# Sixteen weight-block sums of a seven-product first layer: from VectorE subtractions to ScalarE copies plus adding DMA transfers

## The chip, the core and the metric

The kernel runs on one core of one Trainium2 chip. The metric is the device time of one execution in microseconds. Five engines work side by side, each through its own list of instructions in order: TensorE (matrix products, PE in the profile, with its weight loads as PEld), VectorE (DVE), ScalarE (ACT), GpSimd (POOL) and SyncE (SP). They wait for each other through semaphores. SP and POOL also issue DMA transfers here; all of these run on the core's 16 DMA engines.

## What is computed

Block-sorted attention (4 batches, 8 heads, sequence 768, head size 64) is followed by four small two-layer networks ("experts") whose outputs are mixed by token weights. The change is in the experts' first layer, `x @ w1[e]`:

```python
def _moe_ref(x, domain_probs, w1, w2):
    p = domain_probs / (domain_probs.sum(-1, keepdims=True) + 1e-09)
    out = np.zeros((N, D), dtype=np.float32)
    for e in range(E):
        h = np.maximum(x @ w1[e], 0.0)
        out += p[:, e:e + 1] * (h @ w2[e])
```

Here x, the attention's output, has 3072 rows (tokens) of 512, each w1[e] is 512 x 1024, each w2[e] 1024 x 512.

## The kernel before, in words

The 3072 tokens are worked through in 12 groups of 256, three ("chunks") to a batch. Groups 0 to 5 (batches 0 and 1) compute the first layer with plain products (line 768). In their chunks the attention of the next batch is woven in. Groups 6 to 11 (`last_chunk`, from G0 = 6 on) have no attention left and compute the first layer of each expert with seven products of half-size blocks instead of eight (the Strassen-Winograd scheme, `seven`, line 1022). For that each weight matrix is cut into four blocks, a11, a12, a21, a22 (each 128 partitions x 1024 f16 values, 2 x 512), and four sums of blocks per expert are wanted once, before group 6: s1 = a21 + a22, s3 = a11 - a21, s2 = s1 - a11, s4 = a12 - s2. The first three go into blocks of the tile `arena`, whose earlier contents (keys, values, queries, mixing matrices of the attention) are no longer needed by then; s4 overwrites a21 in the weight tile itself, so it must wait until the plain first layer of group 5 has read a21. The matching sums of the tokens (t1 to t4) are made by `token_sums` for each group.

The products of `seven` are called by number: p1 (a11 x b11) and p5 (s1 x t1) of expert 0 are issued by `last_begin` near the end of group 5, p6 (s2 x t2) in the middle of that group's last product; p7 uses s3, p4 uses a22 and p3 uses s4. They accumulate in PSUM banks X, Z, Q.

What sets the order of the work: every engine's list is in program order, and the program is an order written out by hand. `chunk(b, c, slot)` calls `slot()` after each of eight first-layer groups (slots 0 to 7) and then after each product of the second layer (slots 8 to 14). At each slot, `PLANS` names attention steps (`st_v`, `st_k`, `st_s`, `st_a`, `st_x`, ...) and, in batch 1, `PLAN_A` names weight sums: an entry (c, n, e, m) is "chunk c, slot n, expert e, sum m", run after the attention steps of the slot. In the second layer of a chunk of batch 1 (lines 826 to 854) ScalarE empties the PSUM banks: line 831 copies bankA to p1 (in the list after slot 9), 834 bankQ to p5, 839 bankA to u2, 844 bankC to ob; TensorE overwrites bankA twice more in the chunk, and each time needs the copy ahead of it to be done. Attention step `st_s` ends in exponentials on ScalarE (line 413), `st_v` in a copy (line 360) and six SP transfers that build vs (line 368), which `st_a` (line 441 on TensorE, 422 and 423 on VectorE) reads; `st_x` issues DMA transposes (line 457).

The sums themselves are made by `input_sums`, one VectorE instruction each (line 968). Fifteen are in `PLAN_A`; the s4 of expert 3 is made in two halves inside group 6 (`late_sums`, lines 1107, 1108 and 1180). In groups 6 to 11 GpSimd does half of the weighting of the hidden layer (line 1045), and ScalarE the rectifying before it (line 1044) and the copies 1052, 1059 and 1067.

Of the kernel before, what the change touches and what calls it, by code (L numbers as in the profile page):

```python
# [12 lines left out]
ALU = mybir.AluOpType  # L13
# [4 lines left out]
def kernel(  # L18
# [11 lines left out]
    nc = tc.nc  # L30
# [916 lines left out]
    def a_block(n):  # L947
        return arena[:, ds(n * AW, AW)].rearrange("p (k f) -> p k f", k=2)


    A_ORDER = (6, 7, 8, 0, 1, 2, 3, 4, 5, 9, 10, 11)
    As = []
    for e in range(E):
        w, hk, hf = w1sb[e], NKC // 2, FF // 2
        As.append({
            "a11": w[:, 0:hk, 0:hf], "a12": w[:, hk:NKC, 0:hf],
            "a21": w[:, 0:hk, hf:FF], "a22": w[:, hk:NKC, hf:FF], "s4": w[:, 0:hk, hf:FF],
            "s1": a_block(A_ORDER[3 * e]), "s3": a_block(A_ORDER[3 * e + 1]), "s2": a_block(A_ORDER[3 * e + 2]),
        })

    def input_sums(e, n, half=None):
        a = As[e]
        dst, x, y, op = (
            ("s1", "a21", "a22", ALU.add), ("s3", "a11", "a21", ALU.subtract),
            ("s2", "s1", "a11", ALU.subtract), ("s4", "a12", "s2", ALU.subtract),
        )[n]
        part = slice(None) if half is None else slice(half, half + 1)
        nc.vector.tensor_tensor(a[dst][:, part], a[x][:, part], a[y][:, part], op)

    Bs = {}  # L970

    G0 = 2 * (R // 2)
    GN = B * (R // 2)

    def token_sums(g):

        b, c = divmod(g, R // 2)
        xT = xTs[b].rearrange("p k i x -> p k (i x)")
        blk = lambda k, t: xT[:, ds(2 * k, 2), ds((2 * c + t) * P, P)]
        t3 = kTs[g % 2][:, 0:3 * 2 * P].rearrange("p (n k x) -> p n k x", n=3, k=2)  # L980
        t = Bs[g] = {
            "b11": blk(0, 0), "b12": blk(0, 1), "b21": blk(1, 0), "b22": blk(1, 1),
            "t1": t3[:, 0], "t2": t3[:, 1], "t3": t3[:, 2],
            "t4": wide[g % 2][:, 0:2 * P].rearrange("p (k x) -> p k x", k=2),
        }
        for dst, x, y in (("t1", "b12", "b11"), ("t2", "b22", "t1"), ("t3", "b22", "b12"), ("t4", "b21", "t2")):
            nc.vector.tensor_tensor(t[dst], t[x], t[y], ALU.subtract)

    last = {}

# [31 lines left out]
    def seven(g, e):  # L1022

        a, t, pb = As[e], Bs[g], pbs[divmod(g, R // 2)]
        X, Z, u2, u3, t22, t12 = [last[nm][e % 2] for nm in ("X", "Z", "u2", "u3", "t22", "t12")]
        X, Z, Q = X[:], Z[:], last["Q"][e][:]
        tt = nc.vector.tensor_tensor

        def product(dst, lhs, rhs, first=False):
            for f in range(KH):  # L1030
                for k in range(2):
                    nc.tensor.matmul(  # L1032
                        dst[:, ds(f * P, P)], a[lhs][:, k, ds(f * P, P)], t[rhs][:, k, :],
                        start=(first and f == 0 and k == 0), stop=(f == KH - 1 and k == 1), skip_group_check=True,
                    )

        def finish(i, j, src):
            nc.vector.scalar_tensor_tensor(
                out=Hb[:, e, ds(i * KH, KH), ds(j * P, P)], in0=src.rearrange("p (f x) -> p f x", f=KH), scalar=0.0,
                op0=ALU.max, in1=pb[:, ds(e, 1), ds(j * P, P)].broadcast_to([P, KH, P]), op1=ALU.mult,  # L1040
            )

        def finish2(i, j, src):
            nc.scalar.activation(src, src, AF.Relu, bias=0.0, scale=1.0)  # L1044
            nc.gpsimd.tensor_tensor(  # L1045
                Hb[:, e, ds(i * KH, KH), ds(j * P, P)], src.rearrange("p (f x) -> p f x", f=KH),
                pb[:, ds(e, 1), ds(j * P, P)].broadcast_to([P, KH, P]), ALU.mult,
            )

        def p1():  # L1050
            product(Z, "a11", "b11", True)
            nc.scalar.copy(X, Z)  # L1052

        def p5():
            product(Q, "s1", "t1", True)

        def p6():
            product(X, "s2", "t2")
            nc.scalar.copy(u2, X)  # L1059

        def p2():
            product(Z, "a12", "b21")
            finish(0, 0, Z)

        def p7():
            product(X, "s3", "t3")
            nc.scalar.copy(u3, X)  # L1067
            tt(t22, Q, u3, ALU.add)  # L1068

        def p4():  # L1070
            product(X, "a22", "t4")
            finish(1, 0, X)

        def p3():
            product(Q, "s4", "b22")
            tt(t12, Q, u2, ALU.add)  # L1076

        return {
            1: p1, 2: p2, 3: p3, 4: p4, 5: p5, 6: p6, 7: p7,
            22: lambda: finish2(1, 1, t22), 12: lambda: finish2(0, 1, t12),  # L1080
        }
# [6 lines left out]
    def last_chunk(g):  # L1088
# [6 lines left out]
        for e in range(1, E):  # L1095
            now, prev = prs[e], prs[e - 1]
            now[1]()
            prev[7]()
            if e > 1:
                prs[e - 2][12]()  # L1100
            now[5]()
            now[2]()
            now[6]()
            prev[22]()
            prev[4]()
            prev[3]()
            for n in late_sums.pop((g, e), ()):
                input_sums(*n)
        now[7]()
        prev[12]()  # L1110

# [47 lines left out]
        if not final:  # L1159
            token_sums(g + 1)  # L1160
# [12 lines left out]


    PLAN_A = [
        (1, 11, 0, 0), (1, 13, 0, 1), (2, 1, 0, 2), (2, 3, 1, 0), (2, 5, 1, 1), (2, 7, 1, 2),
        (2, 8, 2, 0), (2, 9, 2, 1), (2, 10, 2, 2), (2, 10, 0, 3), (2, 11, 1, 3), (2, 11, 3, 0), (2, 12, 2, 3),
        (2, 13, 3, 1), (2, 14, 3, 2),
    ]
    late_sums = {(G0, 1): [(3, 3, 0)], (G0, 2): [(3, 3, 1)]}  # L1180


    mk0 = mix_half("k", 0, 0, psm, 8)
# [109 lines left out]
    for b in range(2):  # L1293
        for c in range(R // 2):
            done = (1, 2) if (b, c) == (0, 0) else ()
            at = [2 * len(done)]

            def slot(b=b, c=c, at=at):
                here = (c, at[0])
                for cc, n, f, *args in PLANS[b]:  # L1300
                    if (cc, n) == here:
                        f(*args)
                if b:
                    for cc, n, e, m in PLAN_A:
                        if (cc, n) == here:
                            input_sums(e, m)
                    if here == (R // 2 - 1, 7):
                        prepare_last()
                    if here == (R // 2 - 1, 12):
                        token_sums(G0)  # L1310
                    if here == (R // 2 - 1, 13):
                        last_begin(G0)
                at[0] += 1

            chunk(b, c, slot, done)
    for g in range(G0, GN):
        last_chunk(g)
# [28 lines left out]
```

The softmax here doesn't subtract the row's maximum and nothing guards it: scores larger than these inputs give would overflow.

## Time and profile before

| | |
|---|---|
| median of 4 runs | 365.7 us (364.48 to 366.11) |
| the profiled execution | 365.25 us, span 363.2 us |
| TensorE busy / VectorE / ScalarE / GpSimd | 354.8 / 280.1 / 157.6 / 117.4 us |
| the 17 instructions of line 968 | from 178.9 to 220.3 us; a whole one 0.68 us, the two halves 1.08 and 0.81 |
| granted TensorE clock | 1.000 |

The span goes from the first to the last instruction of one profiled execution; its time is a little longer. "Busy" is the time in which an engine has an instruction under way; register, semaphore and DMA-issuing instructions are not counted. Matmuls are pipelined, so a busy TensorE is not one at its peak. In a view in order of time a row gives start and length in us, the engine, the line of the kernel, the operation, out<-in, shapes and count; rows of one kind that follow each other are merged. An idle stretch ahead of a row and what ended it stand in brackets. DMA queue rows give packets, MB and their share of 16 engines' span; issue rows give the KB of one transfer and the median time in us from issue to landing.

### The profile page before, as it was taken

What the parts mean: (1) busy time and instruction counts of PE and PEld (TensorE: products, weight loads), DVE (VectorE), ACT (ScalarE), POOL (GpSimd) and SP (SyncE); (2) the same over time, 40 slices, a digit from 0 to 9 for tenths busy, and PEclk for the clock granted to TensorE, in tenths of its full rate; (3) what the DMA queues carried; (4) which work ended last, traced back from release to release, by engine and by line L of the source; (5) the groups of instructions that cost most, each with busy time, mean ns of one, the idle gap of its engine ahead of it and who ended that gap; (6) DMA issues with size and microseconds to landing.
All of it is one profiled execution on the core that took longest, in us unless ns stands there. A gap on an engine that the chain in (4) does not pass through costs nothing.

```text
span 363.2 us, 10556 instructions
## 1 busy us (share of the span) xinstructions
PE 354.8 (98%) x4517; PEld 315.0 (87%) x4517; DVE 280.1 (77%) x559; ACT 157.6 (43%) x282; POOL 117.4 (32%) x134
## 2 busy tenths in 40 slices
PE   8899999999999999999999999999999999999996
PEld 8786858788888888988888899999999998999995
DVE  5654898769788676866799979968779679588694
ACT  2664330451423355366400157165283382571740
POOL 8872011735112430000000018137055083180470
PEclk9999999999999999999999999999999999999999
DMA  7999999999999999935450210310202202101101
GB/s 102 206 207 230 210 209 201 201 193 188 198 127 145 200 120 173 164 73 74 91 125 2 58 60 4 58 60 3 88 31 43 77 2 60 60 2 64 56 15 44
DMA packets 69753, 38.34 MB, mean 106 GB/s; under 512 B 40390, under 2 KB 64716, under 8 KB 69708
## 3 DMA queue, kind: packets, MB, share of 16 engines
q0 software_dynamic: 34640, 17.83, 37.6%
q1 hardware_dynamic: 35068, 19.85, 26.8%
q8 instruction: 35, 0.57, 0.7%
q14 instruction: 10, 0.08, 0.1%
HBM read 42.00 MB, written 6.34 MB: 133 GB/s over the span
## 4 chain that ended last, share of the span: by engine, by line
PE 75%; DMA 16%; DVE 6%; issue 1%; ACT 1%; POOL 1%; DVEq 0%; SPq 0%; POOLq 0%; ACTq 0%
PE ps_Q L1121 20%; PE ps_h L768 15%; PE ps_p L753 13%; PE ps_X L1032 9%; DMA arena<-in_q_dram 7%; DMA w<-in_moe_w_dram 6%; PE ps_Q L1032 6%; PE ps_Z L1032 6%; DMA qT<-arena 2%; PE ps_s L406 1%; PE ps_a L441 1%; DVE Hb L774 1%; PE ps_k L387 1%; PE ps_Q L753 1%; DVE xsl L423 1%
## 5 line engine op out<-in xcount | busy, mean ns | idle before, releaser
L1045 POOL TENSOR_TENSOR Hb<-tmp,pb 128x512 f16<-128x512 f32 x48 | 61.9, 1296 | 150.5 <-ACT tmp L1044 148.8
L768 PE MATMUL ps_h<-xT,w 128*128 128x256 f16 x672 | 78.4, 273 | 0.0
L768 PEld LDWEIGHTS <-w 128*128 128x128 f16 x672 | 64.5, 98 | 8.5
L774 DVE SCALAR_TENSOR_TENSOR Hb<-ps_h,pb 128x1024 f16<-128x1024 f32 x42 | 51.3, 1222 | 18.8 <-PE ps_h L768 18.6
L1032 PEld LDWEIGHTS <-w 128*128 128x128 f16 x768 | 46.6, 98 | 0.8
L1121 PEld LDWEIGHTS <-Sb 128*128 128x128 f16 x384 | 37.2, 98 | 4.1
L1032 PEld LDWEIGHTS <-arena 128*128 128x128 f16 x576 | 34.7, 98 | 0.1
L1044 ACT ACTIVATE tmp<-tmp 128x512 f32<-128x512 f32 x48 | 30.5, 635 | 6.4 <-DVE tmp L1076 5.2
L753 PEld LDWEIGHTS <-Sb 128*128 128x128 f16 x288 | 27.4, 98 | 4.2 <-issue 0.7
L1121 PEld LDWEIGHTS <-Hb 128*128 128x128 f16 x288 | 27.4, 98 | 2.9
L413 ACT ACTIVATE ET<-ps_s 96x768 f16<-96x768 f32 x24 | 18.0, 802 | 27.3 <-PE ps_s L406 27.0
L1032 PE MATMUL ps_X<-kT,arena 128*128 128x128 f16 x384 | 29.3, 219 | 0.0
L121 POOL DMA_DIRECT2D arena<-in_q_dram x24 | 19.9, 838 | 27.3 <-DMA qT<-arena 17.2
L396 ACT CAST kT<-ps_k 64x384 f16<-64x384 f32 x48 | 22.7, 473 | 13.3 <-PE ps_k L387 12.3
L739 DVE TENSOR_TENSOR Sb<-Hb 128x512 f16<-128x512 f16 x45 | 26.4, 607 | 0.0
L1068 DVE TENSOR_TENSOR tmp<-ps_Q,tmp 128x512 f32<-128x512 f32 x24 | 16.6, 691 | 12.2 <-ACT tmp L1067 8.0
L1121 PE MATMUL ps_Q<-w,Sb 128*128 128x256 f16 x192 | 24.7, 273 | 0.0
L1121 PE MATMUL ps_Q<-w,Hb 128*128 128x256 f16 x192 | 23.9, 273 | 0.0
L1052 ACT COPY ps_X<-ps_Z 128x512 f32<-128x512 f32 x24 | 13.7, 570 | 22.9 <-PE ps_Z L1032 22.4
L753 PEld LDWEIGHTS <-Hb 128*128 128x128 f16 x216 | 20.6, 98 | 3.1 <-issue 0.3
L1121 PE MATMUL ps_Q<-T,Sb 128*128 128x256 f16 x192 | 22.9, 273 | 0.0
L1059 ACT COPY tmp<-ps_X 128x512 f32<-128x512 f32 x24 | 14.1, 585 | 12.2 <-PE ps_X L1032 12.2
(189 smaller groups left out, 606.5 us busy)
## 6 DMA issues: line engine op xcount, KB each, us to landing
w<-in_moe_w_dram POOLq DMA_DIRECT2D x7, 1024.0 KB, 27.3
pb<-p_dram SPq DMA_DIRECT2D x12, 512.0 KB, 5.8
arena<-in_k_dram POOLq DMA_DIRECT2D x8, 384.0 KB, 8.6
arena<-in_v_dram POOLq DMA_DIRECT2D x8, 384.0 KB, 8.6
vs<-arena SPq DMA_DIRECT2D x36, 66.0 KB, 5.4
arena<-in_q_dram POOLq DMA_DIRECT2D x24, 96.0 KB, 7.8
out_dram<-ob SPq DMA_DIRECT2D x9, 256.0 KB, 2.0
out_dram<-oa SPq DMA_DIRECT2D x8, 256.0 KB, 2.4
```

The lines of the kernel that those rows point to most:

```text
L121: nc.gpsimd.dma_start(t[:, h // 2, :, h % 2, :], q[b, h].rearrange("(t p) d -> p t d", p=P))
L396: nc.scalar.copy(kT[ds(D * hh, D), r], pk[ds(D * r, D), hh].rearrange("p a (i c) -> p a i c", c=CP),)
L413: nc.scalar.activation(ETs[2 * (pr % 2) + hh][:, 0:S].rearrange("c (a x) -> c a x", a=2), pss[hh][0:BLK, :, 0:HS], AF.Exp, bias=0.0, scale ...
L739: tt(sm[0], blk(0, 1), blk(1, 1), ALU.add)
L753: nc.tensor.matmul(ps, lhs(e, f), Ts[e][rhs][:, f, :], start=(first and e == es[0] and f == 0), stop=(done and e == es[-1] and f == KH - 1 ...
L768: nc.tensor.matmul(ps[:, f, :], w1sb[e][:, kc, ds((4 * g + f) * P, P)], xT[:, kc, ds(2 * c * P, 2 * P)], start=(kc == 0), stop=(kc == NKC ...
L774: nc.vector.scalar_tensor_tensor(out=Hb[:, e, ds(4 * g, 4), :], in0=ps[:], scalar=0.0, op0=ALU.max, in1=pb[:, ds(e, 1), :].broadcast_to([P ...
L1032: nc.tensor.matmul(dst[:, ds(f * P, P)], a[lhs][:, k, ds(f * P, P)], t[rhs][:, k, :], start=(first and f == 0 and k == 0), stop=(f == KH - ...
L1044: nc.scalar.activation(src, src, AF.Relu, bias=0.0, scale=1.0)
L1045: nc.gpsimd.tensor_tensor(Hb[:, e, ds(i * KH, KH), ds(j * P, P)], src.rearrange("p (f x) -> p f x", f=KH), pb[:, ds(e, 1), ds(j * P, P)].b ...
L1068: tt(t22, Q, u3, ALU.add)
L1121: nc.tensor.matmul(ps, lhs(e, f), Ts[e][rhs][:, f, :], start=(first and e == 0 and f == 0), stop=(e == E - 1 and f == KH - 1), skip_group_ ...
```

## The change

The sums leave VectorE. Each is now made in two steps: ScalarE copies one operand to the destination with a sign of +1 or -1 (`nc.scalar.mul`), and then a DMA transfer issued from GpSimd adds the other operand to it, SBUF to SBUF (`accum_op=ALU.add`). Since a copy can change the sign and a transfer can only add, s3 is made as -a21 + a11, and s2 is replaced by its negative, n2 = -s1 + a11; the token sum t2 is replaced by its negative in the same way, so that p6 has the same value, and s4 = n2 + a12. The sums are placed at other slots (the first at chunk 1, slot 8 instead of 11), all sixteen are in `PLAN_A`, `late_sums` and the halves are gone, and experts 2 and 3 exchange their places in `arena`. The n2 copy reads s1, and the s4 copy reads n2, each after its transfer has landed. Nothing else changes.

```diff
-    A_ORDER = (6, 7, 8, 0, 1, 2, 3, 4, 5, 9, 10, 11)
+    A_ORDER = (6, 7, 8, 0, 1, 2, 9, 10, 11, 3, 4, 5)
...
-            "s1": a_block(A_ORDER[3 * e]), "s3": a_block(A_ORDER[3 * e + 1]), "s2": a_block(A_ORDER[3 * e + 2]),
+            "s1": a_block(A_ORDER[3 * e]), "s3": a_block(A_ORDER[3 * e + 1]), "n2": a_block(A_ORDER[3 * e + 2]),
...
-    def input_sums(e, n, half=None):
+    def input_sums(e, n):
+
         a = As[e]
-        dst, x, y, op = (
-            ("s1", "a21", "a22", ALU.add), ("s3", "a11", "a21", ALU.subtract),
-            ("s2", "s1", "a11", ALU.subtract), ("s4", "a12", "s2", ALU.subtract),
+        dst, x, sign, y = (
+            ("s1", "a21", 1.0, "a22"), ("s3", "a21", -1.0, "a11"), ("n2", "s1", -1.0, "a11"), ("s4", "n2", 1.0, "a12"),
         )[n]
-        part = slice(None) if half is None else slice(half, half + 1)
-        nc.vector.tensor_tensor(a[dst][:, part], a[x][:, part], a[y][:, part], op)
+        nc.scalar.mul(a[dst], a[x], sign)
+        nc.gpsimd.dma_start(a[dst], a[y], accum_op=ALU.add)
...
-            "t1": t3[:, 0], "t2": t3[:, 1], "t3": t3[:, 2],
+            "t1": t3[:, 0], "n2": t3[:, 1], "t3": t3[:, 2],
...
-        for dst, x, y in (("t1", "b12", "b11"), ("t2", "b22", "t1"), ("t3", "b22", "b12"), ("t4", "b21", "t2")):
-            nc.vector.tensor_tensor(t[dst], t[x], t[y], ALU.subtract)
+        for dst, x, y, op in (
+            ("t1", "b12", "b11", ALU.subtract), ("n2", "t1", "b22", ALU.subtract),
+            ("t3", "b22", "b12", ALU.subtract), ("t4", "b21", "n2", ALU.add),
+        ):
+            nc.vector.tensor_tensor(t[dst], t[x], t[y], op)
...
-            product(X, "s2", "t2")
+            product(X, "n2", "n2")
...
-            for n in late_sums.pop((g, e), ()):
-                input_sums(*n)
...
     PLAN_A = [
-        (1, 11, 0, 0), (1, 13, 0, 1), (2, 1, 0, 2), (2, 3, 1, 0), (2, 5, 1, 1), (2, 7, 1, 2),
-        (2, 8, 2, 0), (2, 9, 2, 1), (2, 10, 2, 2), (2, 10, 0, 3), (2, 11, 1, 3), (2, 11, 3, 0), (2, 12, 2, 3),
-        (2, 13, 3, 1), (2, 14, 3, 2),
+        (1, 8, 0, 0), (1, 8, 1, 0), (1, 10, 0, 1), (1, 10, 1, 1), (1, 12, 0, 2), (1, 12, 1, 2), (1, 13, 2, 0),
+        (2, 0, 2, 1), (2, 2, 2, 2), (2, 4, 3, 0), (2, 5, 3, 1), (2, 7, 3, 2),
+        (2, 9, 0, 3), (2, 9, 1, 3), (2, 10, 2, 3), (2, 12, 3, 3),
     ]
-    late_sums = {(G0, 1): [(3, 3, 0)], (G0, 2): [(3, 3, 1)]}
```

## Prediction

> **What bounds the kernel now.** I read the busy shares of the page, then busy time by stretch around the changed code, then TensorE's order of time there, then ScalarE's.
>
> ```profile
> span 363.2 us, 10556 instructions
> ...
> PE 354.8 (98%) x4517; PEld 315.0 (87%) x4517; DVE 280.1 (77%) x559; ACT 157.6 (43%) x282; POOL 117.4 (32%) x134
> ```
>
> TensorE is busy for 98% of the span. The changed sums run from 178.9 to 221 us. By stretch (start:end, length, then busy us and instructions of PE, PEld, DVE, ACT, POOL; granted clock, DMA share, GB/s):
>
> ```profile
> 178.00:186.00 8.00, 7.90 (x107) 6.86 (x106) 7.19 (x20) 1.88 (x3) 0.00 (x0) 1.00 0.28 73
> 186.00:202.00 16.00, 16.00 (x148) 14.20 (x146) 15.51 (x22) 0.00 (x0) 0.00 (x0) 1.00 0.22 48
> 202.00:214.00 12.00, 12.00 (x137) 10.96 (x136) 10.60 (x26) 3.22 (x8) 0.00 (x0) 1.00 0.22 65
> 214.00:226.00 12.00, 12.00 (x196) 11.67 (x193) 10.75 (x17) 9.27 (x17) 8.05 (x7) 1.00 0.03 12
> ```
>
> VectorE is nearly full (15.51 of 16 us), yet TensorE idles 0.10 us in 48, at full clock. Pipelined matmuls can hide short waits inside "busy", so I compare the distances of their starts (columns: start, length, ..., count):
>
> ```profile
> 183.55 0.92 PE L441 MATMUL ps_a<-vs,ET 96*128 96x65 f16 x16
> 184.31 14.19 PE L768 MATMUL ps_h<-xT,w 128*128 128x256 f16 x128
> ...
> 217.69 0.61 PE L1032 MATMUL ps_X<-kT,arena 128*128 128x128 f16 x8
> 218.14 0.61 PE L1032 MATMUL ps_X<-ET,w 128*128 128x128 f16 x8
> 218.68 0.61 PE L1032 MATMUL ps_Q<-xT,w 128*128 128x128 f16 x8
> ```
>
> Sixteen 256-wide matmuls take 1.91 us elsewhere and one lasts 0.273, so they start every 1.64/15 = 0.109 us. At that pace 128 need 127 x 0.109 + 0.27 = 14.13 us; the row has 14.19, so the chunk's whole first layer loses 0.06 us beside the full VectorE. Products of eight start 0.45 apart; from 218.14 to 218.68 it is 0.54, so 0.09 is lost, and 0.09 again before 220.55. The L441 product took 0.92 us where the others take 0.65: 0.27 lost. TensorE sets the end, and VectorE's sums hold it up hardly at all.
>
> **What is removed.** Fifteen whole sums of 0.68 us and two halves, 12.1 us of VectorE. The halves are dear, since they run beside GpSimd's products of line 1045:
>
> ```profile
> 216.94 1.08 DVE L968 TENSOR_TENSOR w<-w,arena 128x512 f16<-128x512 f16 x1
> ...
> 220.34 0.81 DVE L968 TENSOR_TENSOR w<-w,arena 128x512 f16<-128x512 f16 x1
> ```
>
> Each is followed by one of the 0.09 us gaps, which I take as theirs: -0.18. The first layer's loss goes too: -0.06. The 0.27 at L441 stays: the VectorE work ahead of it (lines 847, 848, 422, 423 from 181.57 on) starts after an idle stretch of 0.64 us, so no earlier sum delays it. Sum of the gains: **0.24 us**. The other end: all that TensorE's starts lose between 178 and 225 us, 0.69 us.
>
> **What is added on ScalarE.** Sixteen copies of 128x1024 f16. No such row exists. The 512-wide copies take 0.57 to 0.59, the 768-wide ACTIVATE 0.80, and the one 96x1024 copy (line 515) 1.01: I take 1.0 each, and 0.9 from start to start, since two 768-wide ones take 1.50 together. ScalarE's order of time in the chunk where they begin:
>
> ```profile
> 170.71 0.80 ACT L360 CAST arena<-ps_v 128x768 f16<-128x768 f32 x1
> 172.45 0.37 ACT L831 COPY p<-ps_p 128x256 f32<-128x256 f32 x1 [0.95 <-PE ps_p L753]
> 174.69 0.37 ACT L834 COPY p<-ps_p 128x256 f32<-128x256 f32 x1 [1.86 <-PE ps_p L753]
> 175.13 1.50 ACT L413 ACTIVATE ET<-ps_s 96x768 f16<-96x768 f32 x2
> 176.99 0.37 ACT L839 COPY u<-ps_p 128x256 f32<-128x256 f32 x1 [0.35 <-PE ps_p L753]
> ```
>
> Two copies (slot 8) follow 171.5 and end by 173.4; line 831 then ends at 173.8, and TensorE overwrites its bank only at 175.03. Two more (slot 10) follow the exponentials, 176.63 to 178.5; line 839 ends at 178.9, its bank is overwritten at 179.56. Cost nothing, with 0.7 us to spare; a copy 0.4 us longer would still fit. The exponentials of slot 12 (179.72 to 181.22) come ahead of its copies. After that ScalarE is empty until 202.30 (the row 831 there waited 21.1 us), so the ten copies listed between the exponentials and line 831 fit by count: 10 x 0.9 in 21 us.
>
> **What is added on the DMA queues.** Sixteen transfers of 256 KB, issued by GpSimd, whose own work rests until 216.47; its DMA issues take 0.74 to 0.86 in other rows, 13 us for all sixteen. Nothing but these is queued there. No adding transfer is in the trace. The rows around:
>
> ```profile
> q0 software_dynamic: 34640, 17.83, 37.6%
> q1 hardware_dynamic: 35068, 19.85, 26.8%
> ...
> arena<-in_k_dram POOLq DMA_DIRECT2D x8, 384.0 KB, 8.6
> ```
>
> Time of service S: q1, plain, moves 19.85 MB in 0.268 x 363.2 = 97 us of all engines, so 256 KB take 1.3 us; q0, which casts and so reads twice what it writes, 17.83 MB in 137 us, so 2.0 us. An adding transfer also reads twice what it writes: I take 2.0; the ends are 1.3 and 4.0 (the cast's rate once more for the sum). Time L to landing: 3.6 is the least for 96 KB, 5.0 the least and 8.6 the median for 384 KB, 13.1 for the 512 KB pieces that queue up. I take 5.0, and 7.0 where one neighbour of 2.0 is ahead.
>
> **The new waits, on ScalarE.** The copy of n2 reads s1 after its transfer, that of s4 reads n2 after its own. The long chain: s1 of expert 2 is copied 183.0 to 184.0 and lands at 184.0 + L1; n2 of expert 2 and s1 of expert 3 (1.9) end at 185.9 + L1; that lands at 185.9 + L1 + L2; n2 of expert 3 and s4 of experts 0 and 1 (2.7) let line 831 start at 188.6 + L1 + L2. Queued behind it on ScalarE are lines 834, 839, 844, 1052, each awaited by TensorE. Line 831 needs 0.37, and TensorE overwrites its bank at 203.79: no stall while L1 + L2 is at most 14.8. I take 7.0 + 5.0 = 12.0: hidden, with 2.8 us to spare. With 8.6 twice it is 2.4 us late, with 13.1 twice 11.4; with 5.0 twice 4.8 us are spare. The remaining transfers are early: s4 of expert 3 is copied at 207.9, would land by 217.5 even with 8.6, and is first used at 224.97.
>
> A rule of the Trainium skill speaks against the move: "SBUF — State Buffer", section "SBUF: two separate sides", says that a GpSimd-issued transfer starves while VectorE holds the shared port in a 2-port mode. Here GpSimd's 16 issues of line 110 took 740 to 815 ns each in chunks with a busy VectorE; the section "Who interferes with whom" also keeps two-input sums out of that mode. By the first rule each issue might wait out a VectorE instruction, 1.22 us for line 774, which would make L1 + L2 14.4, still no stall; by the second it stays at 12.0. "DMA: Bandwidth & Descriptors", section "Anatomy of one DMA", gives 2.0 us + bytes/436e3, an estimate of 2.6 us for 256 KB, by which nothing waits; its 2.9 for 384 KB lies under the 5.0 measured here.
>
> **Sum.** The profiled execution: 365.25 us, 2.05 around its span of 363.2. Minus 0.24: 365.0. The median shown, 365.7, lies 0.45 above it, so **365.5**. About 0.3% (1.1 us) is what a measurement of this kernel tells from no change.
>
> **Rivals.**
> 1. *ScalarE held by landings (slower).* If S is over about 2.5, the queue itself is late: s1 of expert 3 is the tenth transfer of a queue that starts near 174.4, so it lands at 175.5 + 10 S, line 831 starts 2.7 later, and TensorE waits 10 S - 25.2: nothing at 2.5, 4.8 us at S = 3 (370.3), 14.8 at S = 4 (380.3). Transposes (line 457) and a store fill the DMA engines at 183 to 189 us, just in the chain's first wait, which speaks for it; the 21 empty us of ScalarE and the low DMA share after 190 speak against.
> 2. *The first transfers delay vs.* Six SP transfers of line 368 (issued 171.5 to 174.7, landing in at most 3.7, so 178.5) feed the L441 product at 181.32, with 2.8 to spare. Two sums put wholly in front take 2 x 2.0 = 4.0: 1.2 late, 366.7. Packets of two queues should share, which speaks against the full price.
> 3. *VectorE's relief is worth all of the 0.69:* 365.0, still no measurable change. Only 0.24 has a sum beside it.
>
> **Chances.** Forecast (hidden, 364.9 to 366.6): 0.50; rival 3: 0.08; rival 1: 0.34; rival 2 at a full price: 0.05; a gain over 1.1 us, for which TensorE shows no room: 0.03. So faster 0.03, same 0.58, slower 0.39. Range: from 364.9; upwards it takes in rival 1 up to S = 3.1, 365.5 + 5.8 = 371.3; beyond lie some 0.15.
>
> **What would show it.** Right: no TensorE wait on ScalarE between 186 and 214, line 831 in the second chunk still near 202.3, sums landing in 5 to 7 us, the two 0.09 gaps gone, VectorE some 12 us less busy. Wrong: ScalarE copies waiting for a DMA into 200 us and line 831 after 203.4 (rival 1); L441 after 181.32 (rival 2); a 128x1024 copy well over 1.4 us.

## The result, and the profile after

The changed kernel is slower. Its median is 366.27 us (44 runs, 364.69 to 369.8) against 364.8 us (63 runs, 363.65 to 368.54): ratio 1.0042, 95% interval 1.003 to 1.0054, so about 1.5 us. The prediction said 365.5 and no measurable change: a shift of -0.24 us from a baseline of 365.7, where the measured shift is +1.5 from 364.8. That 366.27 still lies among the forecast's 364.9 to 366.6 is luck, since the baseline came out 0.9 lower.

The profiled execution of the changed kernel took 369.8 us with a span of 368.0. It is the longest of the 44, so its sizes are to be read with the second profile below (365.62 us). TensorE ran at half clock in two stretches of it; the first, near 17 us, lies long before the change, and the profiles of two experiments (early, s4_past) show it too.

The page's first lines, after:

```profile
span 368.0 us, 10600 instructions
...
PE 358.0 (97%) x4517; PEld 317.3 (86%) x4517; DVE 270.1 (73%) x542; ACT 172.8 (47%) x298; POOL 136.9 (37%) x150
```

VectorE has 10.0 us less (280.1 before). The prediction had 12.1, the sum of the rows' lengths; but these rows overlap their neighbours a little, and busy time counts an overlap once. ScalarE has 15 more, GpSimd 20 more. None of this tells why it is slower. The stretches around the changed code do (start:end, length, then busy us and instructions of PE, PEld, DVE, ACT, POOL; granted clock, DMA share, GB/s):

```profile
186.00:202.00 16.00, 16.00 (x148) 14.23 (x147) 13.60 (x19) 3.04 (x4) 6.03 (x5) 1.00 1.12 149
202.00:204.00 2.00, 2.00 (x21) 1.80 (x19) 0.00 (x0) 0.53 (x1) 0.00 (x0) 1.00 1.10 200
204.00:206.00 2.00, 0.99 (x10) 0.74 (x8) 0.00 (x0) 2.00 (x3) 1.18 (x2) 1.00 0.59 169
206.00:208.00 2.00, 0.81 (x8) 0.73 (x8) 1.29 (x4) 1.91 (x4) 2.00 (x3) 1.00 0.83 120
208.00:210.00 2.00, 2.00 (x12) 1.43 (x11) 2.00 (x7) 0.01 (x1) 1.67 (x2) 0.52 1.07 149
210.00:212.00 2.00, 2.00 (x13) 1.52 (x12) 0.71 (x4) 0.36 (x1) 0.00 (x0) 0.63 1.18 168
212.00:214.00 2.00, 2.00 (x21) 1.78 (x20) 0.00 (x0) 1.33 (x2) 0.00 (x0) 1.00 0.62 89
```

Two things are new. Between 204 and 208 us TensorE has a hole (0.99 and 0.81 of 2 us). From 208 to 212 it is "busy" all the time, but at 0.52 and 0.63 of its clock: 12 and 13 matmuls in 2 us where the full clock has 21. In the stretch from 186 to 202 the DMA share has risen from 0.22 to 1.12 (packets overlap, so it can exceed one). TensorE's order of time names what ended the hole:

```profile
185.39 14.14 PE L768 MATMUL ps_h<-xT,w 128*128 128x256 f16 x128
...
203.08 1.91 PE L753 MATMUL ps_Q<-w,Sb 128*128 128x256 f16 x16
207.19 2.76 PE L753 MATMUL ps_p<-T,Sb 128*128 128x256 f16 x16 [2.20 <-DVE oa L832]
209.74 2.76 PE L753 MATMUL ps_p<-T,Hb 128*128 128x256 f16 x16
...
222.75 0.61 PE L1035 MATMUL ps_X<-kT,arena 128*128 128x128 f16 x8
223.20 0.61 PE L1035 MATMUL ps_X<-ET,w 128*128 128x128 f16 x8
223.65 0.61 PE L1035 MATMUL ps_Q<-xT,w 128*128 128x128 f16 x8
```

The first layer takes 14.14 us instead of 14.19, and the products start 0.45 apart where 0.54 stood before (line 1032 of before is 1035 here): the gains came. At 207.19, though, TensorE waited for line 832, VectorE's instruction after the ScalarE copy of line 831; it reads bankB, which stands in one PSUM tile with bankA. Sixteen matmuls then take 2.76 us instead of 1.91: the half clock. ScalarE's order of time tells what kept line 831:

```profile
182.21 2.00 ACT L967 ACTIVATE arena<-arena 128x1024 f16<-128x1024 f16 x2
184.10 2.00 ACT L967 ACTIVATE arena<-w 128x1024 f16<-128x1024 f16 x2
194.93 1.06 ACT L967 ACTIVATE arena<-arena 128x1024 f16<-128x1024 f16 x1 [8.84 <-issue]
195.89 1.99 ACT L967 ACTIVATE arena<-w 128x1024 f16<-128x1024 f16 x2
203.47 1.06 ACT L967 ACTIVATE arena<-arena 128x1024 f16<-128x1024 f16 x1 [5.59 <-DMA arena<-w]
204.43 1.99 ACT L967 ACTIVATE w<-arena 128x1024 f16<-128x1024 f16 x2
206.32 0.35 ACT L831 COPY p<-ps_p 128x256 f32<-128x256 f32 x1
```

By the program order the row at 194.93 is the n2 copy of expert 2, which needs s1 of expert 2 to have landed (the profile found no releaser and puts "issue"); the one at 203.47 is n2 of expert 3 and waits for s1 of expert 3, by name of its transfer. ScalarE's list is in order, so line 831, whose data were ready, stood behind both. The first s1 was copied until 185.15, the second until 196.93: L1 = 194.93 - 185.15 = 9.8 and L2 = 203.47 - 196.93 = 6.5 us, 16.3 together. The prediction had allowed 14.8.

### The profile page after: what moved, and what is told of

It reads as the page before. It is cut to its first block, busy times and chain, and to the rows that moved or that the text cites. A ratio compares the mean times of both kernels' runs of the same rounds, so it can differ in the third digit from the quotient of the medians.

```text
span 368.0 us, 10600 instructions
## 1 busy us (share of the span) xinstructions
PE 358.0 (97%) x4517; PEld 317.3 (86%) x4517; DVE 270.1 (73%) x542; ACT 172.8 (47%) x298; POOL 136.9 (37%) x150
## 4 chain that ended last, share of the span: by engine, by line
PE 81%; DMA 10%; DVE 4%; issue 1%; POOL 1%; SPq 1%; ACT 1%; ACTq 0%; DVEq 0%; POOLq 0%
PE ps_Q L1122 20%; PE ps_h L768 13%; PE ps_p L753 11%; PE ps_X L1035 9%; PE ps_Q L1035 6%; PE ps_Z L1035 6%; DMA arena<-in_v_dram 3%; PE ps_h L661 3%; DMA room<-arena 3%; PE ps_o L696 3%; PE ps_p L803 2%; DMA vs<-arena 2%; DMA arena<-w 2%; PE ps_s L406 1%; PE ps_a L441 1%
## 5 line engine op out<-in xcount | busy, mean ns | idle before, releaser
L968 POOL DMA_DIRECT2D arena<-w x12 | 14.5, 1488 | 50.6 <-PE ps_a L441 33.0
```

## The balance on TensorE

From the distances of TensorE's starts, as in the prediction, I add up all that is lost between 178 and 225 us: 0.69 us before, 2.82 after (2.36 of it in the wait at 207.19). Without that wait 0.46 is left, so the gain is 0.69 - 0.46 = 0.23, the predicted 0.24. The half clock is not in this sum. The same 350 matmuls that hold the wait, from the 2250th to the 2600th start of TensorE, took 32.76 us before and 36.73 after; kernels without any wait take 32.71 there. So after costs 36.73 - 32.71 = 4.02: 2.36 of waiting and 1.66 of half clock, which is half of a stretch of 3.4 us (0.48 and 0.37 missing in two stretches of 2 us make 1.70).

Behind the 1750th start TensorE loses nothing elsewhere. Up to the 2000th, from there to the 2250th, and from the 4000th to the last, the starts take 21.29, 19.72 and 40.70 us before and after alike; from the 2600th to the 4000th before needs 102.23 and every other kernel 102.06, which is the two gaps again. The first 1750 starts, where the kernels are alike, took 1.1 us more in the profiled changed kernel (143.8 against 142.75, with the half clock near 17 us); so much of its span is not the change's.

One more difference lies outside the span. A run's time is on average 2.07 us longer than its span in before and in the two experiments without adding transfers (2.01 to 2.14), and 1.78 in the changed kernel and every experiment with them (1.72 to 1.85). So 0.29 us more are gained, which the prediction did not have. They go with the adding transfers; why, no run shows.

## Experiments

**The changed kernel again (after_again).**

> The changed kernel once more, for a second profile. Theory T (ScalarE's list): line 831 of batch 1's last chunk stands behind the n2 copy of expert 3 and two s4 copies, which wait for landings, and TensorE waits for line 831. The wait in an ordinary run should then be 1 to 2 us at the product after bankQ, and where it reaches some 2 us a stretch of half clock follows. Theory R (shared resources: DMA engines, SBUF, GpSimd's descriptors) expects the loss spread over many places, none over 0.5 us. Time 1 to 2 us over before by both.

Measured: 366.1 us, ratio 1.0026 (0.9999 to 1.0053). TensorE's waits from 178 to 225 us, and then ScalarE's order of time:

```profile
PE ps_p L753 <- DVE oa L832: 1.4, 1, 1.4
```

```profile
192.61 1.06 ACT L967 ACTIVATE arena<-arena 128x1024 f16<-128x1024 f16 x1 [8.22 <-issue]
...
200.96 1.06 ACT L967 ACTIVATE arena<-arena 128x1024 f16<-128x1024 f16 x1 [4.63 <-DMA arena<-w]
201.92 1.99 ACT L967 ACTIVATE w<-arena 128x1024 f16<-128x1024 f16 x2
203.81 0.35 ACT L831 COPY p<-ps_p 128x256 f32<-128x256 f32 x1
```

The same wait at the same place, 1.55 us by the starts; L1 + L2 = 9.2 + 6.3 = 15.5. The clock stayed at 1.0. So the wait belongs to the change, and of these two profiles only the one with the longer wait has the half clock. In 9 of the 44 runs of the changed kernel the mean clock was 0.995 or less (median 368.97 us). That alone does not tell of the wait, since 15 of the 94 runs of the kernel before beside the experiments have it too (median 366.00). The runs with a higher clock have a median of 366.02 after and 364.69 before: 1.3 apart, where 1.55 - 0.24 - 0.29 = 1.0 is due by this one profile's wait.

**Line 831 ahead of the chain's end (past831).** n2 of expert 3 and the s4 copies ahead of line 831 go behind it:

```diff
-        (2, 0, 2, 1), (2, 2, 2, 2), (2, 4, 3, 0), (2, 5, 3, 1), (2, 7, 3, 2),
-        (2, 9, 0, 3), (2, 9, 1, 3), (2, 10, 2, 3), (2, 12, 3, 3),
+        (2, 0, 2, 1), (2, 2, 2, 2), (2, 4, 3, 0), (2, 5, 3, 1),
+        (2, 10, 3, 2), (2, 10, 0, 3), (2, 11, 1, 3), (2, 11, 2, 3), (2, 14, 3, 3),
```

> The n2 copy of expert 3 and the four s4 copies are listed behind line 831 (slots 10, 11 and 14 instead of 7, 9, 10 and 12); every copy and transfer stays. T: no TensorE wait at that place, line 831 back right after its product, time 0 to 0.4 us under before (ratio 0.999 to 1.000). R: the same copies and transfers cost the same, 1 to 2 us over before (ratio 1.003 to 1.005).

Measured: 364.63 us, ratio 0.9976 (0.9952 to 1.0). ScalarE's order of time:

```profile
193.89 1.06 ACT L967 ACTIVATE arena<-arena 128x1024 f16<-128x1024 f16 x1 [8.87 <-issue]
194.86 2.18 ACT L967 ACTIVATE arena<-w 128x1024 f16<-128x1024 f16 x2
202.26 0.37 ACT L831 COPY p<-ps_p 128x256 f32<-128x256 f32 x1 [5.22 <-PE ps_p L753]
```

The first landing is as late as ever (9.8), but line 831 now waits for TensorE, as it did before the change, and TensorE for nobody. All sixteen copies and transfers are still made. The whole loss lies in the place of three copies in ScalarE's list, n2 of expert 3 and the first two of s4 (the other two that the edit moves stood behind line 831 already).

**The long landing itself made shorter (early).** s1 of expert 2 is listed ahead of n2 of experts 0 and 1:

```diff
-        (1, 8, 0, 0), (1, 8, 1, 0), (1, 10, 0, 1), (1, 10, 1, 1), (1, 12, 0, 2), (1, 12, 1, 2), (1, 13, 2, 0),
+        (1, 8, 0, 0), (1, 8, 1, 0), (1, 10, 0, 1), (1, 10, 1, 1), (1, 12, 2, 0), (1, 12, 0, 2), (1, 12, 1, 2),
```

> Only s1 of expert 2 is moved, ahead of the two n2 copies of slot 12 (it was behind them, slot 13). Its copy starts 1.9 us earlier and its transfer has two neighbours of some 2 us fewer ahead of it. T: the chain and line 831 come 4 to 6 us earlier, so the wait of 1 to 2.4 us is gone, ratio 0.999 to 1.000. R: as the changed kernel, 1.003 to 1.005.

Measured: 364.21 us, ratio 0.9965 (0.994 to 0.9991), no wait. ScalarE:

```profile
181.75 1.05 ACT L967 ACTIVATE arena<-w 128x1024 f16<-128x1024 f16 x1
...
189.15 1.06 ACT L967 ACTIVATE arena<-arena 128x1024 f16<-128x1024 f16 x1 [3.52 <-issue]
190.11 1.04 ACT L967 ACTIVATE arena<-w 128x1024 f16<-128x1024 f16 x1
196.83 1.06 ACT L967 ACTIVATE arena<-w 128x1024 f16<-128x1024 f16 x1 [5.67 <-DMA room<-arena]
199.93 1.06 ACT L967 ACTIVATE arena<-arena 128x1024 f16<-128x1024 f16 x1 [2.04 <-DMA arena<-w]
```

With no neighbour ahead L1 is 189.15 - 182.80 = 6.35 instead of 9.8: two neighbours cost 3.4 us. The chain also starts earlier by their two copies, 1.9. Some of it is given back: the second transfer, issued at 191.47, now has four others ahead of it in the queue, the last of them with packets until 197.9, so it lands late (199.93 - 191.15 = 8.8 instead of 6.5). The copy of s3 of expert 3 waits for the transposes, since they still read its destination. 1.9 + 3.4 - 2.3 = 3.0: line 831 starts at 202.82, in time (3.5 under 206.32, since TensorE's first 1750 starts took 0.5 less in this profile).

**s4 behind line 831 (s4_past).** The two s4 copies that stood between the chain and line 831 go behind it:

```diff
-        (2, 9, 0, 3), (2, 9, 1, 3), (2, 10, 2, 3), (2, 12, 3, 3),
+        (2, 10, 0, 3), (2, 10, 1, 3), (2, 11, 2, 3), (2, 12, 3, 3),
```

> Only the s4 copies are moved behind line 831 (experts 0 and 1 to slot 10, expert 2 to slot 11); the n2 copy of expert 3 with its wait stays ahead of it. T: line 831 comes two copies (1.9 us) earlier, so of a wait of 1.5 to 2.4 us 0 to 0.5 us is left and no half clock follows; ratio 0.999 to 1.001. If the wait were not made by what stands ahead in ScalarE's list, nothing changes: 1.003 to 1.004.

Measured: 364.05 us, ratio 0.9976 (0.9954 to 0.9997). n2 of expert 3 starts at 202.44, line 831 at 203.40, and TensorE waits for nothing: here 2 x 0.95 us of copies decide.

**How much a sum costs on VectorE (no_sums).** Before, with its seventeen sums left out:

```diff
-        nc.vector.tensor_tensor(a[dst][:, part], a[x][:, part], a[y][:, part], op)
+        return
```

> The kernel before with its VectorE sums left out altogether (the seven products then read whatever the blocks held). It bounds what VectorE's relief can be worth. The prediction's sum: 0.24 us under before, ratio 0.9993. If the relief is worth more than the start distances of the matmuls show, the ratio is under 0.998.

Measured: 364.66 us, ratio 0.9986 (0.996 to 1.0012); 0.45 us lost by the starts, as in every kernel without the wait. More than 0.24 was not to be had from VectorE's sums by any move of them that the starts can show.

**The transfers left out, the copies kept (no_adds).**

```diff
-        nc.gpsimd.dma_start(a[dst], a[y], accum_op=ALU.add)
```

> The changed kernel without the adding transfers: the sixteen ScalarE copies stay, the sums are left out. T: with no landing to wait for, the copies are done well before 202 us, no wait at line 831, ratio 0.998 to 1.000. If ScalarE's load alone were the cost, it stays at 1.002 to 1.005.

Measured: 364.4 us, ratio 0.9992 (0.9976 to 1.0009); line 831 starts after 8.75 us of rest on ScalarE. The copies cost nothing; the landings do.

**The copies left out, the transfers kept (adds_only).**

```diff
-        nc.scalar.mul(a[dst], a[x], sign)
```

> The changed kernel without the sixteen ScalarE copies: the adding transfers stay and add to whatever the blocks held. T: the DMA load alone holds nothing, no TensorE wait over 0.3 us between 178 and 226 us, ratio 0.998 to 1.000. R: the transfers and GpSimd's descriptor writing cost by themselves, ratio 1.002 to 1.004.

Measured: 369.62 us, ratio 1.0137 (1.0109 to 1.0165): a miss. Nothing on ScalarE now spaces the transfers, so the experiment changed what it was meant to keep. GpSimd's order of time, then TensorE's waits:

```profile
168.38 7.29 POOL L967 DMA_DIRECT2D arena<-w  x6 [7.11 <-DMA qT<-arena]
```

```profile
PE ps_a L441 <- DMA vs<-arena: 4.2, 1, 4.2
```

Six sums are issued in one row instead of two by two and run beside the six transfers that build vs; TensorE waits 4.4 us by the starts for them, and half a clock follows (186.3 to 189.7). This is the mechanism of the prediction's rival 2. In the changed kernel it does not act, since the copies spread the same six issues from 173.85 to 186 us. It says nothing on the price of the landings that it was made for.

**The transposes taken away (no_x).** Two of the DMA transposes of the last batch (line 457) are replaced by a memset:

```diff
     def st_x(b, pr):
...
+        if b == B - 1 and pr >= 2:
+            nc.vector.memset(xTs[b][:, pr], 0.0)
+            return
```

> The changed kernel without the DMA transposes of batch 3's last two head pairs; a VectorE memset of zeros stands in their place (that part of x is left out). It asks why the first landing took 9 to 10 us. If the transposes share the DMA engines with the sums from 184 to 196 us, the service of one sum falls from 2.1 to 3.1 us to 1.8, s1 of expert 2 lands about 2 us earlier, and the wait is 0 to 0.3 us. If the queue's own order (two neighbours ahead, 2.5 us from issue to first packet) makes it all, the wait stays at 1.5 us or more.

Measured: 365.04 us, ratio 1.0008 (0.9996 to 1.002), between the expectations. The wait falls from 1.55 (after_again, the like-clocked profile) to 0.92, L1 from 9.2 to 8.3. These two transposes are a part of the long landing, not its cause.

**The wait made longer (later).** s1 of expert 3 is listed behind s3 of expert 3, which waits for the transposes:

```diff
-        (2, 0, 2, 1), (2, 2, 2, 2), (2, 4, 3, 0), (2, 5, 3, 1), (2, 7, 3, 2),
+        (2, 0, 2, 1), (2, 2, 2, 2), (2, 4, 3, 1), (2, 5, 3, 0), (2, 7, 3, 2),
```

> The changed kernel with s1 and s3 of expert 3 exchanged in the list, so that s1's copy stands behind s3's, which waits for a transpose to free its block. T: s1 of expert 3 is copied some 2.7 us later (195.28 against 193.58 at the start, and one copy more), the n2 copy and line 831 follow, and TensorE's wait grows from 1.5 to 2.4 us to 4 to 5; with it the half clock should come in every run. Time 2.7 to 4.5 us over the changed kernel. R: no difference from the changed kernel, since the same copies and transfers run.

Measured: 369.95 us, ratio 1.0149 (1.0124 to 1.0174). The waits, then the stretches:

```profile
PE ps_p L753 <- DVE oa L832: 4.2, 1, 4.2
```

```profile
204.00:206.00 2.00, 0.00 (x0) 0.00 (x0) 0.00 (x0) 2.00 (x3) 1.19 (x2) 1.00 0.05 16
206.00:208.00 2.00, 0.82 (x5) 0.56 (x5) 1.30 (x4) 1.90 (x4) 2.00 (x3) 0.62 0.84 120
208.00:210.00 2.00, 2.00 (x11) 1.40 (x10) 2.00 (x7) 0.00 (x0) 1.66 (x2) 0.52 1.08 149
```

**The same wait, filled (later_filled).** "later", with 18 unused matmuls (512 wide) on TensorE ahead of the one that waits:

```diff
+            if last:
+                for _ in range(18):
+                    nc.tensor.matmul(last["X"][0][:], w1sb[0][:, 0, 0:P], w1sb[0][:, 1, 0:512], start=True, stop=True)
```

> As later, with 18 matmuls of 512 columns (3.8 us) that nothing uses, put on TensorE just ahead of the product that waits. If the half clock is what follows an idle TensorE, it is gone here, and the time is 1.0 to 1.7 us under later; if it has another cause, the clock falls as in later and the time is that of later or more.

Measured: 367.82 us, ratio 1.0087 (1.0066 to 1.0108). The stretches:

```profile
204.00:206.00 2.00, 2.00 (x11) 0.88 (x10) 0.07 (x1) 2.00 (x4) 1.96 (x3) 1.00 0.16 34
206.00:208.00 2.00, 2.00 (x16) 1.36 (x14) 2.00 (x7) 1.12 (x2) 2.00 (x3) 1.00 1.11 157
208.00:210.00 2.00, 2.00 (x21) 1.78 (x20) 1.93 (x8) 0.37 (x1) 0.89 (x1) 1.00 1.14 159
```

Line 831 is still late (205.54 instead of 206.32), but the clock holds at 1.00, and 2.13 us of the 5.17 over before are gone. Not all of that is the clock's: the unused matmuls hold TensorE 3.88 us by the starts, 0.49 less than the 4.37 of the wait. By the starts from 2250 to 2600 the half clock of "later" costs 38.39 - 32.71 - 4.37 = 1.31, and 1.31 + 0.49 = 1.8 of the 2.13. The mean clock is 0.995 or less in all four runs of later and in none of the four of later_filled. So the half clock follows from the idle stretch and not from the late copy or the transfers.

**Both repairs (both, both_again).** The edits of "early" and "s4_past" together, measured twice:

> All sums as in the changed kernel, with s1 of expert 2 ahead of the n2 copies (as in early) and the s4 copies behind line 831 (as in s4_past): the version with the most room. T: no wait at line 831 in any run, 0.24 us under before (ratio 0.9993), which is less than this measurement tells from no change; over 1 us under the changed kernel.

> The kernel of both once more on another chip run, to see whether it lies under the kernel before. The start distances of its matmuls lose 0.24 us less than before's between 178 and 226 us, which makes a ratio of 0.9993; the first measurement gave 0.998. Expected 0.997 to 1.000; under 0.997 something besides TensorE's waits in this stretch is gained.

Measured: 364.06 us, ratio 0.998 (0.9963 to 0.9996), and 363.84 us, ratio 0.9974 (0.996 to 0.9988). ScalarE in the first of them:

```profile
188.75 1.06 ACT L967 ACTIVATE arena<-arena 128x1024 f16<-128x1024 f16 x1 [3.74 <-issue]
...
199.05 1.06 ACT L967 ACTIVATE arena<-arena 128x1024 f16<-128x1024 f16 x1 [2.08 <-DMA arena<-w]
202.26 0.37 ACT L831 COPY p<-ps_p 128x256 f32<-128x256 f32 x1 [2.15 <-PE ps_p L753]
```

Two us to spare at line 831. The idea of the change, with its copies put elsewhere, beats both kernels: 0.68 and 0.85 us under the runs of before beside it (364.74 and 364.69). TensorE's starts show 0.24 of that, from the first layer and the two gaps, and 0.29 lie outside the span. The remaining 0.15 to 0.3 are within the intervals. The other three versions without the wait (past831, early, s4_past) came out under what was expected, too: the 0.29 makes 0.0008 of their ratios, and the rest is again within the intervals. It cannot be read from single profiles, since the first 143 us, where the kernels are alike, scatter by more: the 1750th start comes between 141.6 and 143.8 us.

## Why the prediction was wrong

**The step that failed** is the landing time of s1 of expert 2: "I take 5.0, and 7.0 where one neighbour of 2.0 is ahead", and with it "I take 7.0 + 5.0 = 12.0: hidden, with 2.8 us to spare". Measured: 9.8 + 6.5 = 16.3, and 9.2 + 6.3 in the second profile. With "early" the missing 4.3 divide so: the landing without a neighbour is 6.35 and not 5.0 (1.35), the neighbours cost 3.4 and not 2.0 (1.4), and the second landing, with n2 of expert 2 just ahead, has 6.5 and not 5.0 (1.5). Three things are in it:

- *Two neighbours, not one.* n2 of experts 0 and 1 are ahead in ScalarE's list, in GpSimd's and in the queue. I had counted one, and of it the queue's service alone.
- *The issue.* I took GpSimd's 0.74 to 0.86 us for one transfer. The row of line 968 in the changed kernel (minimum, median, maximum in ns), and below it the landing from issue:

```profile
L968 POOL DMA_DIRECT2D arena<-w x12: 1176/1468/2014, 173.8 to 204.8; - x12
...
DMA to landing us min/median/max: 3.8/5.4/10.3
```

  The four issues from 183.55 end 1.22 us apart, while ScalarE's copies end 0.95 apart. So the third, s1 of expert 2, is issued by 187.18, 2.0 us after its copy; with 0.8 us an issue it would have been 1.1.
- *The transposes* on the same DMA engines, which SP's row shows from the other side: the two issues that took 2.88 us before take 6.73.

```profile
186.19 6.73 SPq L457 DMA_TRANSPOSE room<-arena  x2
```

**The place was right, the term was not.** The chain, the waiting instruction and the limit of 14.8 were on record, and with 16.3 in them they give 1.5 us of wait. The profiled 2.36 has 0.5 more because TensorE waits for line 832 as well: VectorE's 0.42 us stand between the copy and the release, which the prediction left out. The last 0.35 are copies 1.06 long instead of 1.0 and a chain that began 0.1 later.

**Rival 1** (ScalarE held by landings) is what happened, but not by its formula. It was priced by the service S above 2.5 us, the queue itself being late. S was about right. The queue's row from 172 to 215 us holds the packets of fifteen transfers (272 each); 67.7% of sixteen engines in 43 us make 1.94 us a transfer (2.0 taken):

```profile
q0 software_dynamic: 4080, 3.93, 67.7%
```

By 10 S - 25.2 that is no wait at all. Single transfers differ, though: counted off 272 packets at a time, they had 1.5 to 3.2 us from first to last packet. The longest was n2 of expert 0, the first neighbour in the chain's queue, beside the transposes and the store that the prediction had named as speaking for this rival. What I had treated as two separate matters, S for the rival and L for the forecast, meets in L: with 2.8 us to spare and the two L known only between 5.0 and 13.1, the cover was not safe, and the chance of 0.50 for "hidden" leaned on the low end.

**The half clock** was priced nowhere. A late copy was counted as its wait; in the profiled run a TensorE that idled for 2.4 us then paid 1.7 more.

**What held.** The gain (0.24), the copies (1.04 to 1.06 us, 0.95 from start to start; 1.0 and 0.9 taken), slots 8 to 12 at no cost, vs in time, s4 of expert 3 early. The rule of the Trainium skill that spoke against the move ("SBUF — State Buffer", section "SBUF: two separate sides") showed no effect here: GpSimd's issue took 1.19 us at 204.82, where VectorE had no instruction from 202 to 206, and 1.19 at 183.55, beside VectorE's rows. The issue is long with or without VectorE; whether any of its instructions here holds the shared port, no run tells. The page "DMA: Bandwidth & Descriptors", section "Anatomy of one DMA", by its formula gave an estimate of 2.6 us for 256 KB; the measured least is 3.8, the median 5.4.

## What to carry to other kernels

When a step is moved to an in-order engine that is idle, its new waits are paid by whatever stands behind it in that list: work out the time at which the next awaited instruction must start, follow the chain of landings to it with all neighbours in the issuer's and the queue's list, and put the waiting step behind that instruction unless the slack covers the spread of the landings and not only their median (3.8 to 10.3 us here, with two landings in the chain). Here two lines of an order table turned 1.5 us of loss into some 0.7 to 0.85 of gain, with all the same work done. A wait that leaves TensorE idle for over 2 us can have a second price in the clock.

## What the hardware showed beyond the forecast

- After an idle TensorE the granted clock was half for 3.4 us: after 2.4 us idle (the profiled changed kernel) and after 4.4 us ("later", "adds_only"), not after 1.55 or 0.92 us, and not when unused matmuls filled the 4.4 us. The Trainium skill, "TensorE: Matmul & The Clock Gate", section "Part 1: The HAM clock gate (the "warmup" mystery)", has the clock halved after an idle window of some 3.4 us that runs freely; here 2.4 us were enough once. Where between 1.55 and 2.4 us it begins, and how often, stays open. Length may not be all: in these traces the clock changes on a grid of 3.41 us (at 16.92, 20.33, 208.06 and 211.48 in the changed kernel, 1, 55 and 1 steps apart). The 2.4 us lay within one step (204.65 to 208.06), while in after_again the grid, counted on from its first record at 5.65, has an edge at 203.62 that cuts the 1.55 us in two. The half clock near 17 us, in three profiles, had no idle stretch over 1 us ahead of it.
- An adding transfer of 256 KB between SBUF tiles took 1.18 to 2.01 us to issue on GpSimd, with 1,024 B packets of 120 ns on average (102 in the median), and 3.8 to 10.3 us from issue to landing.
- Two DMA transposes took 6.73 us to issue beside such transfers, 2.88 without.
